# Two private pairs of PSUM banks become one ring of four for the first layer and the attention beside it

## The chip, the cores and the metric

One Trainium2 chip, one of its cores. The metric is device time in microseconds (us): the time of the whole program on that core, median of several executions. Engines are named as the profile names them: PE is TensorE (matmul), PEld its weight load, DVE is VectorE, ACT is ScalarE, SP issues DMAs.

## The reference

Attention with random features for 4 batches, 8 heads and 576 tokens, then two feed-forward layers over all 2304 tokens. Inputs are double precision.

```
def phi(x):
    h = einsum('bhsd,md->bhsm', x, omega) - sum(x * x, -1) / 2
    return exp(h - max(h, -1)) / sqrt(m)
kv  = einsum('bhsm,bhsd->bhmd', phi(k), v);  z = sum(phi(k), axis=2)
x   = (phi(q) @ kv) / (phi(q) @ z + 1e-6)          # to 2304 x 512
h   = x @ w_in                                     # 512 -> 2048
y   = (h * sigmoid(1.702 * h)) @ w_out             # first layer
out = ((y @ w_a) * (y @ w_b)) @ w_out2             # second layer
```

## The kernel before

Every matrix is held as a sum of two half-precision parts, high and low, so a product takes three matmuls (high by high, high by low, low by high). The work runs in this order on one core: the attention of batch 0 alone, then four tiles of 512 tokens of the first layer, then a rest tile of 256 tokens, then the second layer. Beside tile 0 runs the attention of batch 1, beside tile 1 that of batch 2, beside tile 2 that of batch 3. Tile 3 has none beside it. These four stretches are called stages A, B, C and D below.

**A tile of the first layer** (`ffn1`) has 16 h units, numbered f. Unit f is 12 matmuls into one PSUM bank `ph` (L654 to L656), then tanh on ACT (L662, gives `th`), a product on DVE that reads `ph` a second time (L665), a rounding copy on ACT (L671, `gh`) and the rest on DVE (L672, `gl`). The bank is free after L665. Two units later in program order `y_unit` f takes `gh` and `gl` into four accumulators `y` with 12 more matmuls (L685 to L687).

**The attention of a batch** goes by head pairs, k0 to k3 and then q0 to q3 (named k1_2 for batch 1, head pair 2). A pair takes three feature tiles of one PSUM bank `pa` each (L414 and L415: four, four and one slots). From each bank DVE takes the maximum (L480, then L486 makes the bias `nb`), and ACT the exponentials (L446), after which that bank is free. A k pair then sums into one bank of `pa` (L538 and L540 for batch 1, L528 to L530 later) that a copy on ACT empties (L544, or L503 and DVE's L504). A q pair multiplies by that sum (L584) into two banks, which DVE divides (L593 to L598). The attention's matmuls, the weights' conversion (L214, L254, L262 on DVE, L272 on ACT, L221 on DVE) and the h units are written as generators that take turns: `run` steps the tile, then the weights, then `side_step` steps each attention phase that is alive.

**Who sets the order.** The order of instructions on each engine is laid down by the scheduler when the program is built. It goes by the order of the program and by when a tile's buffer comes free: a matmul that opens a bank whose former tenant is not yet read stands behind others that can go. PSUM has eight banks: `ps_acc` holds four for the `y` accumulators, `ps_ring` two for `ph`, `ps_att` two for `pa`. Each of these pools hands out its banks in turn, and each turn waits for that bank's last reader.

```
ps_acc = ctx.enter_context(tc.tile_pool(name="ps_acc", bufs=4, space=PSUM))
ps_ring = ctx.enter_context(tc.tile_pool(name="ps_ring", bufs=2, space=PSUM))
ps_att = ctx.enter_context(tc.tile_pool(name="ps_att", bufs=2, space=PSUM))
```

`head` opens tiles 0 and 1: it takes the first three units, the third into a bank of `ps_acc`.

Of the kernel before, what the change touches and what calls it, by code (L numbers as in the profile page):

```python
# [9 lines left out]
F32 = mybir.dt.float32  # L10
# [23 lines left out]
def fused_kernel(  # L34
# [18 lines left out]
    P = 128  # L53
# [27 lines left out]
    ps_ring = ctx.enter_context(tc.tile_pool(name="ps_ring", bufs=2, space=PSUM))  # L81
    ps_att = ctx.enter_context(tc.tile_pool(name="ps_att", bufs=2, space=PSUM))
# [207 lines left out]
    def w_need(n):  # L290
        while w_done[0] < n:
            w_done[0] = next(w_gen)
# [348 lines left out]
    YS = S_Y / (S_G * S_W)  # L641
    ys = {}

    def ffn1(j, xh, xl, n):

        gh, gl, yacc, phs = {}, {}, {}, {}

        def h_products(f, cs, pool=ps_ring, tag="ring"):
            if f not in phs:
                phs[f] = pool.tile([P, 512], F32, tag=tag, name=f"ph{j}_{f}")  # L650
            ph = phs[f]
            w, fs = w_in[f // 8], slice(f % 8 * P, (f % 8 + 1) * P)
            for c in cs:
                nc.tensor.matmul(ph[:, :n], w[:, 0, c, fs], xh(c), start=(c == 0), stop=False)  # L654
                nc.tensor.matmul(ph[:, :n], w[:, 0, c, fs], xl(c), start=False, stop=False)  # L655
                nc.tensor.matmul(ph[:, :n], w[:, 1, c, fs], xh(c), start=False, stop=(c == KC - 1))  # L656

        def h_unit(f, cs=range(KC)):
            h_products(f, cs)
            ph = phs.pop(f)  # L660
            th = mp.tile([P, 512], F32, tag="f32", name=f"th{j}_{f}")
            nc.scalar.activation(  # L662
                out=th[:, :n], in_=ph[:, :n], func=AF.Tanh, scale=0.5 * 1.702 / (S_X * S_W)
            )
            nc.vector.scalar_tensor_tensor(  # L665
                out=th[:, :n], in0=th[:, :n], scalar=1.0, in1=ph[:, :n], op0=ALU.add, op1=ALU.mult
            )
            GS = 0.5 * S_G / (S_X * S_W)
            a = gp.tile([P, 512], F16, tag="gh", name=f"gh{j}_{f}")
            b = gp.tile([P, 512], F16, tag="gl", name=f"gl{j}_{f}")  # L670
            nc.scalar.activation(out=a[:, :n], in_=th[:, :n], func=AF.Copy, scale=GS)  # L671
            nc.vector.scalar_tensor_tensor(  # L672
                out=b[:, :n], in0=th[:, :n], scalar=GS, in1=a[:, :n],
                op0=ALU.mult, op1=ALU.subtract,
            )
            gh[f], gl[f] = a, b

        def y_unit(f):
            w = w_out[f // 4]
            for c in range(KC):  # L680
                if f == 0:
                    yacc[c] = ps_acc.tile([P, 512], F32, tag="acc", name=f"y{j}_{c}")
                cs = slice(c * P, (c + 1) * P)
                o = yacc[c][:, :n]
                nc.tensor.matmul(o, w[:, 0, f % 4, cs], gh[f][:, :n], start=(f == 0), stop=False)  # L685
                nc.tensor.matmul(o, w[:, 0, f % 4, cs], gl[f][:, :n], start=False, stop=False)  # L686
                nc.tensor.matmul(o, w[:, 1, f % 4, cs], gh[f][:, :n], start=False, stop=(f == FC1 - 1))  # L687

        def main(after=None, first=2):

            following = None
            for f in range(FC1):
                w_need(2 * (f // RW) + 2)
                y_unit(f)
                if f + 1 == FC1:
                    yd = ydram.tile([P, KC, 512], F32, tag=f"y{j}", name=f"yd{j}")
                    for c in range(KC):
                        ye = mp.tile([P, 512], F32, tag="f32", name=f"ye{j}_{c}")
                        nc.scalar.activation(out=ye[:, :n], in_=yacc[c][:, :n], func=AF.Copy, scale=YS)
                        nc.sync.dma_start(out=yd[:, c, :n], in_=ye[:, :n])  # L700
                    ys[j] = yd
                yield
                if first <= f + 2 < FC1:
                    w_need(2 * ((f + 2) // RW) + 1)
                    h_unit(f + 2)
                    yield
                elif f + 2 >= FC1 and after is not None:
                    if following is None:
                        following = after()
                    following[2](f + 2 - FC1)  # L710
                    yield

        return main, h_products, h_unit


# [298 lines left out]


    def psp_att():
        return ps_att.tile([P, 512], F32, tag="att", name="pa")

    rr = [0]

# [94 lines left out]
    def rest_tile():  # L1115
        xTr = zp.tile([P, 2, KC, 2, P], F16, tag="z", name="xTr")
        for r in range(2):
            nc.sync.dma_start_transpose(
                out=xTr[:, :, :, r, :].rearrange("p l c t -> p (l c) t"),
                in_=x16r[:, r].rearrange("p l c t -> p (l c t)"),  # L1120
            )
        return ffn1(
            4,
            lambda c: xTr[:, 0, c].rearrange("p r t -> p (r t)"),
            lambda c: xTr[:, 1, c].rearrange("p r t -> p (r t)"),
            2 * P,
        )
# [2 lines left out]

    def head(tile, units):
        _, products, unit = tile
        for f in range(units):
            w_need(2 * (f // RW) + 1)
            if f < 2:
                products(f, range(KC - 1))
            else:
                products(f, range(KC - 1), ps_acc, "acc")
            yield
        for f in range(units):  # L1140
            unit(f, (KC - 1,))
            yield

    def next_tile(b, make):
        def made():
            finish_side(b)
            following.append(make())
            return following[-1]

        return made  # L1150

    xT = x_tile(0, zp, "z")
    with tc.tile_pool(name="att", bufs=2) as att:
# [28 lines left out]
        with tc.issue_after(own["xt", "q0_2"].ins):  # L1182
            w_steps(POST_W, NW1)
        following.append(ffn1(0, *xparts(xT), SM))
        for b in range(1, B):
            x1 = x_tile(b, zp, "z")
            t0 = (0, 0, 1, -EARLY)[b]
            if b < 3:
                begin_k(b, att, psp_att, t0, AL, b == 1)
            begin_q(b, att, x1, psp_att, t0 + NHP * AL, AL, b == 1)  # L1190
            if b == 2:
                begin_k(3, att, psp_att, 37 - EARLY, AL, False)
            ahead = next_tile(b, lambda: ffn1(b, *xparts(x1), SM))
            if b == 1:
                run(head(following[0], 3), 1, NW1)
                run(following[0][0](first=3), 1, NW1)
                ahead()
            else:
                if b == 2:
                    run(head(following[-1], 3), 11 / 32, NW1 + 2)  # L1200
                run(following[-1][0](ahead, 3 if b == 2 else 2), 11 / 32, (NW1 + 2, NWE)[b - 2])
# [50 lines left out]
```

## Time and profile before

| what | value |
|---|---|
| median of 3 runs | 900.74 us (899.37 to 902.21) |
| the profiled execution | 899.4 us, its span 897.6 us |
| stage A (tile 0, batch 1) | 54.6 to 176.3 us |
| stage B (tile 1, batch 2) | 176.3 to 278.0 us |
| stage C (tile 2, batch 3) | 278.0 to 383.0 us |
| stage D (tile 3 alone) | 383.0 to 468.5 us |
| rest tile and second layer | 468.5 to 897.6 us |
| PE busy | 872.3 us of the span |

The profile is of one execution, 1.3 us below the median of the three. Its span runs from the first instruction to the last. The stage limits are read from the timeline of PE, about where one tile gives way to the next. In the timelines a matmul's length is that of its passage, while the next one starts earlier: matmuls of 512 columns start one after another, at less than their length, so what a matmul costs PE is read from start to start. Of DVE too an instruction starts a little before its forerunner's printed end.

### The profile page before, as it was taken

The page shows a single profiled execution, that of the slowest core. Times are in us where ns is not written, and L with a number is a line of the kernel's source. Part 1 is how long each engine was busy: PE and PEld are TensorE (multiplying, and loading weights), DVE is VectorE, ACT ScalarE, POOL GpSimd, SP SyncE. Part 2 cuts the span into 40 slices and gives each one's busy share as a digit, 9 for nine tenths or more (in the row PEclk, how much of TensorE's full clock was granted, in tenths as well). Part 3 has the DMA queues.
Part 4 walks back from the last instruction along what each step waited for, and adds up shares of the span by engine and source line. Part 5 has one row for each costly group of instructions (what it writes and reads, how often), then busy time and mean ns, then how long its engine had stood idle before and what let it go on. Part 6 is the DMA issues. An engine that isn't in the chain of part 4 may idle for free.

```text
span 897.6 us, 17390 instructions
## 1 busy us (share of the span) xinstructions
PE 872.3 (97%) x7094; PEld 626.3 (70%) x7094; DVE 690.9 (77%) x1244; ACT 455.3 (51%) x1087; POOL 1.4 (0%) x10
## 2 busy tenths in 40 slices
PE   8999999999999999999999999999999999999997
PEld 6864555644554455444448888888888888888886
DVE  5889999778797787999923399777999558566766
ACT  7777774677566776454323354544443122233221
POOL 0000000000000000000000000000000000000000
PEclk9999999999999999999999999999999999999999
DMA  7856895453674323885401055212332022223312
GB/s 205 242 142 162 205 228 197 120 120 82 137 161 110 75 40 67 146 259 222 135 7 49 24 177 175 106 43 83 134 126 83 5 40 84 83 99 125 87 39 71
DMA packets 129343, 105.35 MB, mean 117 GB/s; under 512 B 97776, under 2 KB 111088, under 8 KB 127216
## 3 DMA queue, kind: packets, MB, share of 16 engines
q1 hardware_dynamic: 128558, 103.66, 41.2%
q8 instruction: 55, 0.90, 0.4%
q10 hardware_dynamic: 706, 0.59, 0.2%
q14 instruction: 24, 0.20, 0.1%
HBM read 71.07 MB, written 17.69 MB: 99 GB/s over the span
## 4 chain that ended last, share of the span: by engine, by line
PE 59%; DVE 21%; DMA 7%; ACT 7%; issue 2%; ACTq 0%; SPq 0%; DVEq 0%
PE ph L655 3%; PE ph L654 3%; PE ph L656 3%; PE y L685 3%; PE y L686 3%; PE y L687 3%; DMA xt_k<-x_k 3%; PE oA L904 2%; PE oA L902 2%; PE oA L903 2%; PE pbA L811 2%; PE pbA L809 2%; PE pbA L810 2%; PE paA L809 2%; PE pa L568 2%
## 5 line engine op out<-in xcount | busy, mean ns | idle before, releaser
L686 PE MATMUL y<-gl,w_out 128*128 128x512 f16 (+1 forms) x320 | 114.4, 358 | 0.9 <-DVE gl L672 0.8
L687 PE MATMUL y<-gh,w_out 128*128 128x512 f16 (+1 forms) x320 | 114.2, 358 | 0.0
L685 PE MATMUL y<-gh,w_out 128*128 128x512 f16 (+1 forms) x320 | 111.9, 358 | 0.8 <-ACT gh L671 0.7
L654 PE MATMUL ph<-xT,w_in 128*128 128x512 f16 x256 | 97.1, 379 | 1.5 <-DMA xT<-x_q_3x 0.7
L655 PE MATMUL ph<-xT,w_in 128*128 128x512 f16 x256 | 97.1, 379 | 0.3 <-DVE xT L623 0.3
L656 PE MATMUL ph<-xT,w_in 128*128 128x512 f16 x256 | 97.1, 379 | 0.0
L665 DVE SCALAR_TENSOR_TENSOR th<-th,ph 128x512 f32<-128x512 f32 (+1 forms) x80 | 50.3, 629 | 39.9 <-ACT th L662 39.7
L662 ACT ACTIVATE th<-ph 128x512 f32<-128x512 f32 (+1 forms) x80 | 44.2, 553 | 48.8 <-PE ph L656 48.8
L671 ACT ACTIVATE gh<-th 128x512 f16<-128x512 f32 (+1 forms) x80 | 47.1, 588 | 42.0 <-DVE th L665 41.9
L672 DVE SCALAR_TENSOR_TENSOR gl<-th,gh 128x512 f16<-128x512 f32 (+1 forms) x80 | 50.7, 634 | 15.9 <-ACT gh L671 15.5
L809 PE MATMUL paA<-forms,w_a 128*128 128x256 f16 (+1 forms) x240 | 61.0, 262 | 1.6 <-DVE ca L828 0.8
L809 PE MATMUL pbA<-forms,w_b 128*128 128x256 f16 (+1 forms) x240 | 61.1, 262 | 0.9 <-DVE cb L828 0.9
L811 PE MATMUL pbA<-forms,w_b 128*128 128x256 f16 (+1 forms) x240 | 61.0, 262 | 0.0
L811 PE MATMUL paA<-forms,w_a 128*128 128x256 f16 (+1 forms) x240 | 61.0, 262 | 0.0
L810 PE MATMUL pbA<-forms,w_b 128*128 128x256 f16 (+1 forms) x240 | 61.0, 262 | 0.0
L810 PE MATMUL paA<-forms,w_a 128*128 128x256 f16 (+1 forms) x240 | 61.0, 262 | 0.0
L902 PE MATMUL oA<-w_o,ab 128*128 128x256 f16 x216 | 58.9, 273 | 1.6 <-ACT ab L860 0.9
L904 PE MATMUL oA<-w_o,ab 128*128 128x256 f16 x216 | 58.9, 273 | 0.6 <-DVE ab L861 0.5
L903 PE MATMUL oA<-w_o,ab 128*128 128x256 f16 x216 | 58.9, 273 | 0.0
L817 ACT COPY ka<-paA 128x512 f32<-128x512 f32 (+1 forms) x30 | 16.3, 543 | 78.2 <-PE paA L811 78.1
L910 DVE SCALAR_TENSOR_TENSOR o<-oA,o 128x512 f32<-128x512 f32 (+1 forms) x45 | 28.5, 633 | 34.2 <-PE oA L904 34.2
L687 PEld LDWEIGHTS <-w_out 128*128 128x128 f16 x320 | 31.4, 98 | 29.9 <-issue 3.0
(209 smaller groups left out, 2353.5 us busy)
## 6 DMA issues: line engine op xcount, KB each, us to landing
wraw<-in_moe_w_out_dram SPq DMA_DIRECT2D x14, 1024.0 KB
forms<-fd SPq DMA_DIRECT2D x8, 1792.0 KB
wraw<-in_moe_w_in_dram SPq DMA_DIRECT2D x8, 1024.0 KB
fd<-forms SPq DMA_DIRECT2D x4, 1792.0 KB
wraw<-in_moe_w_a_dram SPq DMA_DIRECT2D x6, 1024.0 KB
wraw<-in_moe_w_b_dram SPq DMA_DIRECT2D x6, 1024.0 KB
vt<-in_v_dram SPq DMA_DIRECT2D x16, 256.0 KB
rawq<-in_q_dram SPq DMA_DIRECT2D x16, 256.0 KB
```

What stands on the lines that cost most here:

```text
L654: nc.tensor.matmul(ph[:, :n], w[:, 0, c, fs], xh(c), start=(c == 0), stop=False)
L655: nc.tensor.matmul(ph[:, :n], w[:, 0, c, fs], xl(c), start=False, stop=False)
L656: nc.tensor.matmul(ph[:, :n], w[:, 1, c, fs], xh(c), start=False, stop=(c == KC - 1))
L685: nc.tensor.matmul(o, w[:, 0, f % 4, cs], gh[f][:, :n], start=(f == 0), stop=False)
L686: nc.tensor.matmul(o, w[:, 0, f % 4, cs], gl[f][:, :n], start=False, stop=False)
L687: nc.tensor.matmul(o, w[:, 1, f % 4, cs], gh[f][:, :n], start=False, stop=(f == FC1 - 1))
L809: nc.tensor.matmul(o[:, i], wh, xh, start=first, stop=False, skip_group_check=True)
L810: nc.tensor.matmul(o[:, i], wh, xl, start=False, stop=False, skip_group_check=True)
L811: nc.tensor.matmul(o[:, i], wl, xh, start=False, stop=final, skip_group_check=True)
L902: nc.tensor.matmul(bank[:, t], lh, wh, start=first, stop=False, skip_group_check=True)
L903: nc.tensor.matmul(bank[:, t], lh, wl, start=False, stop=False, skip_group_check=True)
L904: nc.tensor.matmul(bank[:, t], ll, wh, start=False, stop=final, skip_group_check=True)
```

## The change

`shared()` counts the allocations and hands them to the two pools in turn: the first to `ps_att`, the next to `ps_ring`, and so on. The h units of all tiles and the attention tiles of batches 1 to 3 draw from it, so that the two pairs become one ring of four banks, taken in the order of the program. While `head` runs, `apart[0]` is set and each kind takes its own pool as before. The sums of k pairs and q pairs draw from it too, since they are made by the same `psp_att`. Nothing else is edited. Lines from 641 on move down: L654 to L656 become L667 to L669, L662 L675, L665 L678, L671 L684, L672 L685, L685 to L687 L698 to L700.

```diff
+    taken, apart = [0], [False]
+
+    def shared(own_pool, own_tag, name):
+
+        pool, tag = own_pool, own_tag
+        if not apart[0]:
+            taken[0] += 1
+            pool, tag = ((ps_ring, "ring"), (ps_att, "att"))[taken[0] % 2]
+        return pool.tile([P, 512], F32, tag=tag, name=name)
+
     def ffn1(j, xh, xl, n):
...
-        def h_products(f, cs, pool=ps_ring, tag="ring"):
+        def h_products(f, cs, pool=None, tag=None):
             if f not in phs:
-                phs[f] = pool.tile([P, 512], F32, tag=tag, name=f"ph{j}_{f}")
+                if pool is None:
+                    phs[f] = shared(ps_ring, "ring", f"ph{j}_{f}")
+                else:
+                    phs[f] = pool.tile([P, 512], F32, tag=tag, name=f"ph{j}_{f}")
...
     def psp_att():
-        return ps_att.tile([P, 512], F32, tag="att", name="pa")
+        return shared(ps_att, "att", "pa")
...
     def head(tile, units):
         _, products, unit = tile
+        apart[0] = True
...
         for f in range(units):
             unit(f, (KC - 1,))
             yield
+        apart[0] = False
```

The instructions of both kernels are the same in kind and number on every engine; their order differs. Three places are shown. In the names `th0_4` is unit 4 of tile 0, `mx_k1_2_1` the maxima of batch 1, head pair 2, first group.

DVE in stage A, from `gl` of unit 3 to `gl` of unit 4 of tile 0, before (`wf` is a weight chunk in conversion):

```order
L672 SCALAR_TENSOR_TENSOR gl0_3_1122<-th0_3_1118,gh0_3_1121 128x512
L486 SCALAR_TENSOR_TENSOR nb_k1_1_1_1039<-mh_k1_1_1_1038,sq_k1_1_910 128x4
L262 SCALAR_TENSOR_TENSOR wf5_1080<-wraw5_897,wf5_1080 128x1024
L214 TENSOR_SCALAR wf6_1300<-wraw6_1027 128x1024
L480 TENSOR_REDUCE mx_k1_1_2_1082<-pa_1086 128x1
L665 SCALAR_TENSOR_TENSOR th0_4_1228<-th0_4_1228,ph0_4_1215 128x512
L486 SCALAR_TENSOR_TENSOR mh_k1_1_2_1083<-mx_k1_1_2_1082,sq_k1_1_910 128x5
L254 SCALAR_TENSOR_TENSOR wf6_1300<-wraw6_1027,wf6_1300 128x1024
L486 SCALAR_TENSOR_TENSOR nb_k1_1_2_1084<-mh_k1_1_2_1083,sq_k1_1_910 128x5
L672 SCALAR_TENSOR_TENSOR gl0_4_1232<-th0_4_1228,gh0_4_1231 128x512
```

The same stretch after the change, of whose 25 rows between the two the last ten are shown:

```order
L685 SCALAR_TENSOR_TENSOR gl0_3_1122<-th0_3_1118,gh0_3_1121 128x512
...
L480 TENSOR_REDUCE mx_k1_3_1_1257<-pa_1196 128x4
L486 SCALAR_TENSOR_TENSOR mh_k1_2_2_1190<-mx_k1_2_2_1189,sq_k1_2_977 128x5
L214 TENSOR_SCALAR wf7_1443<-wraw7_1237 128x1024
L486 SCALAR_TENSOR_TENSOR nb_k1_2_2_1191<-mh_k1_2_2_1190,sq_k1_2_977 128x5
L486 SCALAR_TENSOR_TENSOR mh_k1_3_1_1258<-mx_k1_3_1_1257,sq_k1_3_1067 128x4
L254 SCALAR_TENSOR_TENSOR wf7_1443<-wraw7_1237,wf7_1443 128x1024
L486 SCALAR_TENSOR_TENSOR nb_k1_3_1_1259<-mh_k1_3_1_1258,sq_k1_3_1067 128x4
L221 SCALAR_TENSOR_TENSOR w_in0_87<-wf6_1300,w_in0_87 128x4x256
L678 SCALAR_TENSOR_TENSOR th0_4_1228<-th0_4_1228,ph0_4_1215 128x512
L262 SCALAR_TENSOR_TENSOR wf7_1443<-wraw7_1237,wf7_1443 128x1024
L685 SCALAR_TENSOR_TENSOR gl0_4_1232<-th0_4_1228,gh0_4_1231 128x512
```

The product `th0_4` has moved from the fifth place behind `gl0_3` to the 24th. The 25 rows between `gl0_3` and `gl0_4` are 9 of L486, 3 of L480 over 512 elements, 2 of L480 over 128, 7 of the weights' 128x1024 operations with two inputs (L254, L262, L221), 2 of L214, 1 of L403 and 1 of L678. Before, it was 8 rows: 3 of L486, 1 of L480 over 128, 2 with two inputs, 1 of L214 and 1 of L665. On PE, from the first matmul with `gl0_3` to the one with `gl0_4`, there are now 21 matmuls of 512 columns, 34 of 128 columns (L414, L415) and the sums of two k pairs (L538, L540); before it was 22, 2 and none.

PE in stage C, from the last matmul of unit 5 of tile 2 to the first that takes its `gh2_5`, before (rows that repeat are left out):

```order
L656 MATMUL ph2_5_4040<-xT2_2210,w_in0_87 128x512
L685 MATMUL y2_0_3698<-gh2_4_3916,w_out1_90 128x512
L686 MATMUL y2_0_3698<-gl2_4_3917,w_out1_90 128x512
...
L654 MATMUL ph2_6_4173<-xT2_2210,w_in0_87 128x512
...
L414 MATMUL pa_4027<-om_h_93,xt_k3_3_3858 128x128
...
L414 MATMUL pa_4088<-om_h_93,xt_k3_3_3858 128x128
...
L656 MATMUL ph2_6_4173<-xT2_2210,w_in0_87 128x512
...
L656 MATMUL ph2_6_4173<-xT2_2210,w_in0_87 128x512
L685 MATMUL y2_0_3698<-gh2_5_4056,w_out1_90 128x512
L686 MATMUL y2_0_3698<-gl2_5_4057,w_out1_90 128x512
```

And after:

```order
L669 MATMUL ph2_5_4040<-xT2_2210,w_in0_87 128x512
L700 MATMUL y2_3_3710<-gh2_4_3916,w_out1_90 128x512
L528 MATMUL pa_4119<-v16_k3_1_4062,e16_k3_1_3689 128x130
...
L528 MATMUL pa_4119<-v16_k3_1_4062,e16_k3_1_3689 128x65
...
L530 MATMUL pa_4119<-v16_k3_1_4062,e16_k3_1_3689 128x65
L414 MATMUL pa_4157<-om_h_93,xt_k3_3_3858 128x128
...
L414 MATMUL pa_4160<-om_h_93,xt_q3_0_3970 128x128
...
L698 MATMUL y2_0_3698<-gh2_5_4056,w_out1_90 128x512
L698 MATMUL y2_1_3702<-gh2_5_4056,w_out1_90 128x512
...
L699 MATMUL y2_0_3698<-gl2_5_4057,w_out1_90 128x512
```

Before, 24 matmuls of 512 columns and 18 of 128 columns stand between; now one of 512 columns, the 27 of a k pair's sum (L528 to L530) and 10 of 128 columns. The four products with `gh2_5` now come one after another ahead of the first with `gl2_5`.

ACT in stage C, around the tanh and the rounding copy of that unit, before:

```order
L503 ACTIVATE kvh_97<-pa_3986 128x130
L662 ACTIVATE th2_5_4053<-ph2_5_4040 128x512
L518 ACTIVATE v16_k3_2_4195<-vt_133 128x2x260
L518 ACTIVATE v16_k3_2_4195<-vm_134 128x2x65
L671 ACTIVATE gh2_5_4056<-th2_5_4053 128x512
```

And after:

```order
L402 ACTIVATE x16_q3_2_4231<-rawq_3_2_4170 128x9x64
L446 ACTIVATE e_k3_3_0_4083<-pa_4027,nb_k3_3_1_4079 128x128 x4
L675 ACTIVATE th2_5_4053<-ph2_5_4040 128x512
L430 ACTIVATE rawq_3_2_4170<-rawq_3_2_4170 128x576
L684 ACTIVATE gh2_5_4056<-th2_5_4053 128x512
L456 ACTIVATE e16_k3_3_3854<-e_k3_3_0_4083 128x512
```

Between tanh and copy stood two conversions of values and now stands one square (L430); ahead of the tanh there now stand the exponentials of the next head pair.

## Rows read from the trace of the kernel before

**Rows 1.** The page, part 1: busy time, share of the span, count of PE, PEld, DVE, ACT, POOL.
```profile
PE 872.3 (97%) x7094; PEld 626.3 (70%) x7094; DVE 690.9 (77%) x1244; ACT 455.3 (51%) x1087; POOL 1.4 (0%) x10
```

**Rows 2.** Busy time by stage A, B, C, D: window, length, engines (count), clock, DMA share, GB/s.
```profile
54.60:176.30 121.70, 117.64 (x730) 66.89 (x730) 110.56 (x196) 83.38 (x290) 0.00 (x0) 1.00 0.65 176
176.30:278.00 101.70, 98.36 (x742) 50.72 (x741) 84.11 (x195) 71.21 (x176) 0.00 (x0) 1.00 0.59 128
278.00:383.00 105.00, 101.74 (x758) 52.23 (x756) 83.70 (x193) 67.82 (x168) 0.00 (x0) 1.00 0.42 91
383.00:468.50 85.50, 83.93 (x387) 37.61 (x385) 67.86 (x104) 36.07 (x60) 0.00 (x0) 1.00 0.48 157
```

**Rows 3.** Waits of PE, from stages A, B, C, D: waited for, us in total, times, longest.
```profile
PE pa L414 <- ACT e_k L446: 1.7, 1, 1.7
...
PE pa L528 <- DVE sx L248: 0.8, 1, 0.8
...
PE pa L584 <- DMA eqT_q<-e_q: 1.0, 1, 1.0
...
PE ph L654 <- DMA xT<-x_q_3x: 0.7, 1, 0.7
```

**Rows 4.** Timeline of DVE in stage A: start us, length us, line, operation, tiles, shape, count.
```profile
77.49 0.75 DVE L403 SCALAR_TENSOR_TENSOR x_q<-rawq,x_q 128x576 f16<-128x576 f32 x1
...
81.38 0.16 DVE L486 SCALAR_TENSOR_TENSOR nb_k<-mh_k,sq_k 128x4 f32<-128x4 f32 x1
81.45 1.22 DVE L262 SCALAR_TENSOR_TENSOR wf<-wraw,wf 128x1024 int32<-128x1024 int32 x1
82.59 0.69 DVE L214 TENSOR_SCALAR wf<-wraw 128x1024 int32<-128x1024 int32 x1
83.19 0.28 DVE L480 TENSOR_REDUCE mx_k<-pa 128x1 f32<-128x128 f32 x1
83.39 0.68 DVE L665 SCALAR_TENSOR_TENSOR th<-th,ph 128x512 f32<-128x512 f32 x1
...
92.10 0.68 DVE L480 TENSOR_REDUCE mx_k<-pa 128x4 f32<-128x512 f32 x1
```

**Rows 5.** Timeline of PE in stage A, same columns, the wait before an instruction in brackets.
```profile
78.82 0.22 PE L414 MATMUL pa<-om_h,xt_k 128*128 128x128 f16 x1 [1.75 <-ACT e_k L446]
78.88 0.22 PE L415 MATMUL pa<-om_l,xt_k 128*128 128x128 f16 x1
...
82.09 0.38 PE L686 MATMUL y<-gl,w_out 128*128 128x512 f16 x1
82.30 0.38 PE L687 MATMUL y<-gh,w_out 128*128 128x512 f16 x1
...
88.31 1.90 PE L540 MATMUL pa<-vt,e_k 128*128 128x65 f32 x16
90.04 0.38 PE L685 MATMUL y<-gh,w_out 128*128 128x512 f16 x1
```

**Rows 6.** Timeline of PE, then of ACT, around one h unit of stage D.
```profile
450.10 0.38 PE L656 MATMUL ph<-xT,w_in 128*128 128x512 f16 x1
...
450.52 0.60 ACT L662 ACTIVATE th<-ph 128x512 f32<-128x512 f32 x1 [3.36 <-PE ph L656]
...
451.87 0.63 ACT L671 ACTIVATE gh<-th 128x512 f16<-128x512 f32 x1 [0.76 <-DVE th L665]
```

**Rows 7.** Timeline of ACT around one h unit of stage C.
```profile
327.15 0.62 ACT L662 ACTIVATE th<-ph 128x512 f32<-128x512 f32 x1
...
328.76 1.14 ACT L446 ACTIVATE e_q<-pa,nb_q 128x128 f32<-128x128 f32 x4 [0.42 <-DVE nb_q L486]
329.87 0.63 ACT L671 ACTIVATE gh<-th 128x512 f16<-128x512 f32 x1
```

**Rows 8.** Timeline of PE in stage C: first and last matmul of one k-phase sum.
```profile
340.37 0.22 PE L528 MATMUL pa<-v_k,e_k 128*128 128x130 f16 x1 [0.22 <-ACT e_q L446]
...
341.25 0.19 PE L530 MATMUL pa<-v_k,e_k 128*128 128x65 f16 x1
```

## The prediction

> **What bounds the kernel now.** I read the page first: PE is busy for 872.3 us of a span of 897.6, all other engines far less [rows 1]. Then busy time by stage. The change touches stages A to D alone, and there PE is idle for 121.70 − 117.64 = 4.06 us in A, 3.34 in B, 3.26 in C and 1.57 in D, together 12.2 us, at a granted clock of 1.00 in all four [rows 2]. This is a lower bound: matmuls of 512 columns start every 0.215 us while each is printed as 0.38 long (82.09 and 82.30) [rows 5], so a printed matmul covers 0.16 us of a gap behind it. The second thing to see there is DVE: 110.56 us busy of 121.70 in A, so A has two engines near their end, while B and C leave DVE 17 to 21 us. Then PE's waits [rows 3]: few, single, and from different causes. No one wait repeats through a stage.
>
> The profiled execution took 899.4 us, 1.3 below the median of 900.74. The sum is made against 899.4 and 1.3 is added back. A measurement of this kernel can tell about 0.3%, 2.7 us, from no change.
>
> **What the change removes and adds.** No instruction is added or removed, and no DMA; the cost is only in order and waits. The edit of the allocation does three things: it lets attention tiles be opened when both banks of their old pair are unread, it makes an h unit stand behind attention tiles that it never met before, and so it pulls the attention ahead of the h units on PE and on DVE.
>
> *Stage A, unit 4 of tile 0.* The first place shown in the order: between `gl0_3` and `gl0_4` DVE had 8 rows and has 25. From start to start [rows 4] L486 takes 0.07, a two-input 128x1024 operation 82.59 − 81.45 = 1.14, L214 0.60, L480 over 128 elements 0.20; of L403, L665 and L480 over 512 I take the length less the 0.08 that the others overlap: 0.67, 0.60, 0.60. The sum is 9 × 0.07 + 7 × 1.14 + 2 × 0.60 + 2 × 0.20 + 3 × 0.60 + 0.67 + 0.60 = 13.3 us, and 0.68 for `gl0_4`, of L665's shape. DVE is through with `gl0_3` at 81.38 [rows 4] in either kernel, as nothing of the first layer has moved ahead of it, so `gl0_4` is there at 81.4 + 14.0 = 95.4. PE takes `gl0_3` at 82.09, or at 81.5 at the earliest, and then has 21 matmuls of 0.215, 34 of 0.06 (78.82 to 78.88) and two k sums of 1.73 (88.31 to 90.04) and a little more [rows 5]: 10.0 to 10.4 us. It arrives between 91.5 and 92.5 and stands until 95.4. The stall is 2.9 to 3.9; I take **+3.2**. Every matmul behind it waits, since all the work that could be pulled ahead has been.
>
> What hides part of it: batch 1 is through its attention earlier, so DVE is less pressed at the end of the stage. The 1.75 us wait for the exponentials [rows 5] lies before the place, and what it may save is lost again at `gl0_4`. Of the waits behind it I give back 0.7, so A is **+2.5**; the ends are 0 (all 3.2 made up in the stage) and +3.9.
>
> *Stages B and C, the cover of an h unit.* The second place: unit 5 of tile 2 had 24 × 0.215 + 18 × 0.06 = 6.2 us of PE work between its last matmul and the first that takes `gh`. It has now 0.215 + 10 × 0.06 + the k sum, 341.25 − 340.37 + 0.03 = 0.91 [rows 8]: 1.7 us. By the same count units 6 and 7 of that tile have 1.9 and 1.4, and unit 8 of tile 1 has 1.9; units 5 and 6 of tile 1 have 2.5 and 2.7, and the others over 2.8. The chain that has to fit in it is read in stage D, where nothing disturbs it: last matmul at 450.10, so its successor is due at 450.32, and `gh` is written at 451.87 + 0.63 = 452.50 [rows 6], 2.2 us. In stage C it was longer, 327.15 to 330.50 from tanh to copy, 3.35 against 1.98, as exponentials of 1.14 stood between [rows 7], that is 3.6 with the 0.2 ahead of it. At 2.2 the shortfalls of tile 2 are 0.5 + 0.3 + 0.8 = 1.6 us, and of tile 1 0.3. At 3.6 they are 1.9 + 1.7 + 2.2 = 5.8, and 1.7 + 1.1 + 0.9 = 3.7. The third place, ACT's order, shows between tanh and copy only a square of the size of a copy, which DVE's product covers, so I stand near the lower end: C **+2.4**, B **+0.9**. The `gl` are no further loss, as four products with `gh` (0.86) now go ahead of the first with `gl`.
>
> *New waits of the ring.* A matmul that opens an attention bank now waits 15 times for DVE's L678, behind which the next attention tile and all of PE are queued; by the same count four of the 15 have 1.0 to 1.4 us of work against the 1.5 from 450.32 to the end of the product in stage D (tanh at 450.52, copy at 451.87) [rows 6], a shortfall of 1.2 in all. Eleven times an h unit waits for exponentials, with 2.2 us of work or more. Nothing of this is in the trace of before: the ends are 0 and about 3 us, twice the shortfall and some for the exponentials. I take **+1.0**.
>
> *Waits that go.* A k sum (L528) waited 0.8 in B, its cover now being 5 us and more where it was 2 to 3; L584 waited 1.0 in C for the transposed exponentials [rows 3], and these are ready earlier: **−1.8**, 0 at worst. At the start of D a matmul waited 0.7 for the last transposed tile [rows 3]; batch 3 is through some 7 us of PE work sooner: **−0.7**. What might be late next there is DVE, at 67.86 of 85.5 us [rows 2], which I cost at nothing.
>
> The sum: 2.5 + 0.9 + 2.4 + 1.0 − 1.8 − 0.7 = +4.3 by these terms. Each shortfall is taken alone, though a PE that has stood once comes later to the next, and I strike off about a quarter: **+3.3**. That is 902.7 for the profiled execution and **904.0** for the median.
>
> **A rule against this reading.** PE's waits are single and differ [rows 3]; on that I rest the view that more banks have little to give. The Trainium skill, Perfetto Trace Analysis, section Optimization Strategy, says that the same gap repeated on the engine that should be saturated can mean too little PSUM for the next tile. By that rule the ring would take out the gaps; as no gap repeats in a stage here, the trace does not bear it out, and I give it no more than the first rival's chance.
>
> **The rivals.**
>
> *Faster: the bank waits go and the new order holds.* An h unit and the attention each have bursts, and four banks in one ring lend to whichever has one. For it: 12.2 us of idle PE, of which the listed waits that open or close a bank or come behind one are 1.7 + 0.8 + 1.0 + 0.7 = 4.2. Against it: the DVE queue of stage A. If the stall at unit 4 is made up in the same stage (A at −1.7 + 0), chains stay at 2.2 (B and C at +1.9) and the ring's waits are 0, it comes to −1.7 + 1.9 − 2.5 = −2.3, and −4.2 if the shortfalls are covered by PE's being late: 896.5 to 898.4 for the median. It decides if PE's work per stage, which is the same in both, absorbs the stall: PE then waits early and not late.
>
> *No change.* The stall of 3.2 in A replaces other waits of A (4.06 idle in all), and B and C lose 1.9 and win 1.8: 899.5 to 902.5, about 901.
>
> *Slower by more.* Chains in B and C at 3.6 [rows 7] (+9.5), stage A at +3.9, the ring at +3, against −2.5: about +14 at the outside; half the long chains give +9, about **911**. It needs ACT's exponentials to stand ahead of each tanh; they do ahead of unit 5 in the third place.
>
> *The clock falls.* All four stages are at a granted clock of 1.00, 2.4 GHz, with a wait of 1.75 us among them [rows 2, 5], so stalls of 3 us need not lower it. If it fell to 1.2 GHz for 20 us of matmuls, that stretch would take 20 more: about 920. The Trainium skill, TensorE: Matmul & The Clock Gate, section A second HAM failure mode: psum-queue depth-cycling, tells of a kernel whose PE idled between groups as PSUM banks cycled, and whose clock went up and down; the granted clock of before shows none of it [rows 2].
>
> **How the numbers follow.** The forecast, +0.5 to +7 (901.2 to 908), has 0.47; the faster rival 0.21; no change 0.21; slower by more 0.09; the clock 0.02. Of the forecast 0.09 lies below 903.4 and counts as the same. So faster 0.21, same 0.30, slower 0.49. The range leaves out the clock, the far end of the slower rival and the lowest part of the faster: 897 to 911, around 904.0.
>
> **What would show it.** Right: PE idle of some 3 us ahead of `y` of unit 4 of tile 0, released by DVE's L685 or ACT's L684; waits of L698 for L684 in stage C; stage A 2 to 3 us longer, C 1 to 2; no wait of L528 or L584; stage D 0.7 shorter; rest the same. Wrong: stage A as long as before, or no wait at L698. If D or the second layer moved by over 1 us, the cause would be one that I have not named.

## The result and the profile after

| | median | lowest to highest | executions |
|---|---|---|---|
| before | 901.01 us | 899.37 to 902.21 | 4 |
| after | 911.29 us | 906.14 to 916.32 | 4 |

The ratio is 1.0116 (95% interval 1.0094 to 1.0139): 10 us slower. The forecast was 904.0, in a range up to 911. The spread is new too: 10 us between executions where the kernel before has 3. The profiled execution is the quickest of the four, 906.14 us with a span of 904.3; it shows less than the whole loss.

The page of the changed kernel: busy time, then PE and PEclk in 40 slices.

```profile
PE 872.4 (96%) x7094; PEld 629.2 (70%) x7094; DVE 689.2 (76%) x1244; ACT 456.4 (50%) x1087; POOL 1.4 (0%) x10
...
PE   8987899999999999999999999999999999999997
...
PEclk9999999999999999999999999999999999999999
```

PE's work is what it was [rows 1], so the 6.7 us that this span is longer are gaps and slow matmuls. The third, fourth and fifth slices of PE (45 to 113 us) have lost busy time; PEclk, in tenths over 22.6 us, shows nothing yet. Now by stage; each limit lies at the same distance from the tile's last `y` product as before, and the columns are those of [rows 2].

```profile
54.60:184.20 129.60, 118.57 (x730) 68.18 (x728) 114.35 (x204) 90.27 (x300) 0.00 (x0) 0.99 0.65 175
184.20:285.70 101.50, 98.31 (x742) 51.41 (x741) 81.75 (x192) 68.21 (x171) 0.00 (x0) 1.00 0.57 120
285.70:389.00 103.30, 100.26 (x757) 52.87 (x755) 85.66 (x194) 66.63 (x166) 0.00 (x0) 1.00 0.51 113
389.00:475.30 86.30, 84.39 (x389) 37.71 (x388) 62.80 (x98) 34.20 (x55) 0.00 (x0) 1.00 0.36 124
```

Stage A is 129.60 us and was 121.70: +7.9. B is −0.2, C −1.7, D +0.8 [rows 2]. PE is idle for 11.03 us in A where it was for 4.06, and its clock there has a mean of 0.99. So stage A carries all of it. The waits of PE in A, over the stretch of the same limits as before:

```profile
PE pa L538 <- ACT e_k L446: 4.7, 2, 2.9
PE pa L414 <- DMA xt_k<-x_k: 2.0, 1, 2.0
PE pa L414 <- ACT e_k L446: 1.6, 2, 1.1
...
```

The first row was not there before, nor the second; the third is about the one of [rows 3]. Stage D has a row that grew from 0.8 us:

```profile
PE y L699 <- DVE gl L685: 1.8, 4, 0.5
```

**The place.** PE's timeline in tile 0, a wait in brackets:

```profile
81.89 0.38 PE L699 MATMUL y<-gl,w_out 128*128 128x512 f16 x1
...
83.85 0.38 PE L700 MATMUL y<-gh,w_out 128*128 128x512 f16 x1
87.18 0.49 PE L538 MATMUL pa<-vm,e_k 128*128 128x130 f32 x2 [2.95 <-ACT e_k L446]
...
89.40 0.31 PE L414 MATMUL pa<-om_h,xt_k 128*128 128x128 f16 x1
89.51 0.31 PE L415 MATMUL pa<-om_l,xt_k 128*128 128x128 f16 x1
...
90.89 0.27 PE L414 MATMUL pa<-om_h,xt_k 128*128 128x128 f16 x1 [0.43 <-ACT e_k L446]
...
91.05 0.63 PE L667 MATMUL ph<-xT,w_in 128*128 128x512 f16 x1
91.48 0.63 PE L668 MATMUL ph<-xT,w_in 128*128 128x512 f16 x1
...
92.83 0.38 PE L669 MATMUL ph<-xT,w_in 128*128 128x512 f16 x1
93.05 0.38 PE L667 MATMUL ph<-xT,w_in 128*128 128x512 f16 x1
...
96.23 0.49 PE L538 MATMUL pa<-vm,e_k 128*128 128x130 f32 x2 [1.72 <-ACT e_k L446]
...
99.40 0.38 PE L699 MATMUL y<-gl,w_out 128*128 128x512 f16 x1
```

At 83.85 PE has done the products of unit 3. Next in its queue is a sum of k pair 0 (L538), which opens a bank of the ring whose former tenant is a feature tile of k pair 1. It waits 2.95 us for that tile's exponentials. ACT's timeline:

```profile
77.92 1.37 ACT L446 ACTIVATE e_k<-pa,nb_k 128x128 f32<-128x128 f32 x5
...
83.53 0.68 ACT L402 ACTIVATE x_q<-rawq 128x576 f16<-128x576 f32 x1 [0.51 <-DMA xt_k<-x_k]
84.11 1.04 ACT L272 ACTIVATE w_out<-wf 128x1024 f16<-128x1024 f32 x1
85.06 0.24 ACT L422 ACTIVATE rawk<-rawk 128x64 f32<-128x64 f32 x1
...
86.01 1.37 ACT L446 ACTIVATE e_k<-pa,nb_k 128x128 f32<-128x128 f32 x5
...
94.55 0.60 ACT L675 ACTIVATE th<-ph 128x512 f32<-128x512 f32 x1 [0.51 <-PE ph L669]
```

and DVE's, whose bias for them is the first row:

```profile
83.71 0.16 DVE L486 SCALAR_TENSOR_TENSOR nb_k<-mh_k,sq_k 128x5 f32<-128x5 f32 x1
...
91.30 0.89 DVE L480 TENSOR_REDUCE mx_k<-pa 128x1 f32<-128x128 f32 x2 [1.96 <-PE pa L415]
...
95.27 0.68 DVE L678 SCALAR_TENSOR_TENSOR th<-th,ph 128x512 f32<-128x512 f32 x1
...
97.46 0.69 DVE L685 SCALAR_TENSOR_TENSOR gl<-th,gh 128x512 f16<-128x512 f32 x1 [0.37 <-ACT gh L684]
```

Pair 0's own exponentials had ended at 79.29 (the row of 77.92), so the sum does not wait for its own data: it waits for the bank. The bias of pair 1 was there at 83.87. ACT's queue had a conversion ahead of the exponentials that stood 0.51 us for a DMA, a rounding copy of a weight chunk of 1.04 us and four squares; they began at 86.01, and at 87.18 L538 could go.

They are no later than before, however. The same places in the kernel before, PE and then ACT:

```profile
84.66 0.38 PE L656 MATMUL ph<-xT,w_in 128*128 128x512 f16 x1
...
86.60 0.38 PE L656 MATMUL ph<-xT,w_in 128*128 128x512 f16 x1
...
88.03 0.44 PE L538 MATMUL pa<-vm,e_k 128*128 128x130 f32 x2
```

```profile
86.42 1.37 ACT L446 ACTIVATE e_k<-pa,nb_k 128x128 f32<-128x128 f32 x5
```

There the five exponentials began at 86.42 and the first k sum at 88.03, without a wait, since PE had products of an h unit and of `y` to make until then. With the ring the next h products stand behind the attention's banks and begin at 91.05. So the ring did not make the exponentials late; it took away the work that had covered them.

The second k sum waits 1.72 us at 96.23 for exponentials that stand on ACT behind the tanh of 94.55, which itself waits for PE. The product `th0_4` runs at 95.27 and `gl0_4` at 97.46, late as forecast and later, but PE takes `gl0_4` only at 99.40, with no wait: the stalls ahead of it in PE's own queue have used up the time. DVE, which I had working without a gap, itself stood 1.96 us at 91.30 for PE.

**The clock.** In the same rows matmuls of 128 columns start 0.11 us apart from 89.40, and those of 512 columns 0.43 apart at 91.05, against 0.22 at 92.83. The busy time and clock of these stretches:

```profile
84.00:89.00 5.00, 2.05 (x18) 1.82 (x17) 5.00 (x8) 4.57 (x25) 0.00 (x0) 1.00 0.62 213
89.00:93.00 4.00, 3.57 (x20) 2.26 (x20) 2.04 (x8) 2.29 (x7) 0.00 (x0) 0.57 0.12 24
```

Ahead of it PE had been busy for 2.05 of 5 us. Then the granted clock is at its lower level, 1.2 GHz, from about 89 to about 92.5. That stretch costs half its length, some 1.7 us. In the other executions the mean clock is lower: 0.992, 0.992 and 0.986 for 911.32, 911.25 and 916.32 us. With (1 − clock) × span taken off, the four come to 904.3, 904.0, 904.0 and 903.5. So what differs between them is, to 0.8 us, the clock.

### The profile page after: what moved, and what is told of

Read it like the earlier page. It is cut to its first block, busy times and chain, and to the rows that moved or that the text cites. A ratio compares the mean times of both kernels' runs of the same rounds, so it can differ in the third digit from the quotient of the medians.

```text
span 904.3 us, 17397 instructions
## 1 busy us (share of the span) xinstructions
PE 872.4 (96%) x7094; PEld 629.2 (70%) x7094; DVE 689.2 (76%) x1244; ACT 456.4 (50%) x1087; POOL 1.4 (0%) x10
## 4 chain that ended last, share of the span: by engine, by line
PE 59%; DVE 26%; ACT 6%; issue 3%; DMA 3%; ACTq 0%; DVEq 0%; SPq 0%
PE y L699 4%; PE y L698 4%; PE ph L667 4%; PE ph L668 3%; PE ph L669 3%; PE y L700 3%; PE oA L917 2%; PE oA L915 2%; PE oA L916 2%; PE pbA L822 2%; PE pbA L824 2%; PE pbA L823 2%; PE paA L822 2%; DVE gl L685 2%; PE paA L824 2%
## 5 line engine op out<-in xcount | busy, mean ns | idle before, releaser
L699 PE MATMUL y<-gl,w_out 128*128 128x512 f16 (+1 forms) x320 | 114.2, 358 | 2.9 <-DVE gl L685 2.7
L700 PE MATMUL y<-gh,w_out 128*128 128x512 f16 (+1 forms) x320 | 114.3, 358 | 0.0
L698 PE MATMUL y<-gh,w_out 128*128 128x512 f16 (+1 forms) x320 | 110.3, 357 | 1.8 <-ACT gh L684 1.6
L678 DVE SCALAR_TENSOR_TENSOR th<-th,ph 128x512 f32<-128x512 f32 (+1 forms) x80 | 50.5, 631 | 66.6 <-ACT th L675 66.4
L667 PE MATMUL ph<-xT,w_in 128*128 128x512 f16 x256 | 97.3, 380 | 1.5 <-ACT e_q L446 0.9
L669 PE MATMUL ph<-xT,w_in 128*128 128x512 f16 x256 | 97.3, 380 | 0.0
L675 ACT ACTIVATE th<-ph 128x512 f32<-128x512 f32 (+1 forms) x80 | 44.2, 552 | 79.8 <-PE ph L669 78.8
L685 DVE SCALAR_TENSOR_TENSOR gl<-th,gh 128x512 f16<-128x512 f32 (+1 forms) x80 | 50.8, 636 | 17.7 <-ACT gh L684 17.2
L684 ACT ACTIVATE gh<-th 128x512 f16<-128x512 f32 (+1 forms) x80 | 47.0, 588 | 31.4 <-DVE th L678 30.7
L700 PEld LDWEIGHTS <-w_out 128*128 128x128 f16 x320 | 31.3, 98 | 32.9 <-issue 6.0
```

## The experiments

**The change once more.** No edit.

> The changed kernel once more, unedited, for more executions and a second profile. Theory (every execution loses the same 3 us by waits, and the rest by the clock): time plus or minus 0.7 us is 904 + (1 - granted clock) x 909, and in the profile every stretch with a clock under 1.00 lies in stage A behind a stall of PE. Rival (the spread is not the clock's): times of one clock differ by over 2 us, or the low clock lies elsewhere.

Measured: 910.9 us (908.56 to 912.31), ratio 1.0115 (1.0085 to 1.0144). The second profile has the same waits (2.93 and 1.72 at the k sums) and one low stretch, at the same place. By the same subtraction its four executions come to 903.2 to 905.8, up to 1.8 us from the 904 expected where 0.7 was allowed; the clock column has three digits only, and one unit of the last is 0.9 us. Not all of the spread is the clock's: stage C takes 105.3 us in the second profile and 103.3 in the first, both at a clock of 1.00. Over the eight executions of the change the clock takes 6.7 us on average and the rest is 904.2; over 13 of the kernel before it takes 1.7 and the rest is 898.6. Of the 10.6 us between these means some 5.6 are waits and order, then, and some 5 the clock. Where the clock was low in the executions without a profile is not shown.

**The ring without stage A.**

```diff
-    taken, apart = [0], [False]
+    taken, apart, ring = [0], [False], [False]
...
-        if not apart[0]:
+        if ring[0] and not apart[0]:
...
                 ahead()
+                ring[0] = True
```

> The ring is off while tile 0 and batch 1 run (stage A keeps the two pairs) and on from stage B. Theory (the cost is stage A: waits for banks of the ring and a lower clock behind them): stage A as before, granted clock 1.00 throughout, B to D together 0 to 2 us shorter than before, so 899 to 902 us. Rival (the covers of the h units in B and C cost as forecast, 2 to 3 us, and the clock falls there too): 903 us or more. Rival (no part of it matters alone, only the whole): 906 or more.

Measured: 899.03 us, ratio 0.9989 (0.9973 to 1.0005), clock 0.998 to 1.000. From stage B on the ring costs nothing that can be told.

**The ring in stage A alone.** The same flag, the other way round: set at first, cleared behind `ahead()`.

> The ring is on in stage A alone; from tile 1 and batch 2 on the two pairs are back. Theory (stage A is the cost): as slow as the change, 905 to 917 us, granted clock 0.985 to 0.999, tile 0 over some 8 us later than before. Rival (B and C carry the cost): within 2 us of before.

Measured: 913.22 us (909.79 to 920.64), ratio 1.0154 (1.0102 to 1.0206), clock 0.984 to 0.998. Stage A is the cost. Its profiled execution, the slowest and above the range expected, shows a low clock at three places. The first, at some 15 to 33 us, is in batch 0's attention and the last, at 285 us, in tile 1 with the two pairs, neither of which the ring touches; only the second, from 104 us, lies in stage A. There it came behind the second k sum's wait of 1.72 us, and not behind the first's of 2.93.

**PE kept at work where it stood.** Zero weights, so that nothing is added.

```diff
                 y_unit(f)
+                if j == 0 and f == 3:
+                    for i in range(11):
+                        nc.tensor.matmul(
+                            yacc[i % KC][:, :n], own["zero"][:, 0], xh(0), start=False, stop=False
+                        )
...
```

> The change, with eleven matmuls of 512 columns more, zero weights added into the open y accumulator of tile 0 before the last product of unit 3: 2.4 us of PE work where PE stood for 3 us before the first k sum of batch 1; they wait for nothing and add nothing to the result. Theory (the clock falls because PE stood idle there): granted clock 0.998 or more in every run, 903 to 906 us, although there is more work. Rival (the clock falls for another cause, or by the many short gaps around): clock and time as the change, 906 to 917. Rival (the stall is not waiting but lack of order): time up by the 2.4 us.

Measured: 908.42 us (905.21 to 909.99), ratio 1.0085 (1.0054 to 1.0116), clock 0.993 to 0.998. The wait at the first k sum fell from 2.95 to 0.59 us. Its windows, around the first and behind the second k sum:

```profile
84.00:95.00 11.00, 7.85 (x51) 4.72 (x50) 9.33 (x18) 9.17 (x45) 0.00 (x0) 1.00 0.51 148
...
96.00:101.00 5.00, 5.00 (x35) 3.71 (x35) 3.37 (x9) 3.56 (x14) 0.00 (x0) 0.66 0.98 369
```

The clock stays up where it had fallen, and falls some 8 us later, behind the second k sum, whose 1.72 us were left. So the time is in the range of the rival, 906 to 917, and the clock short of the 0.998 expected, though this profile shows the first fall gone. With more of them:

```diff
+                if j == 0 and f == 4 and c == KC - 1:
+                    for i in range(8):
...
+                if j == 0 and f in (2, 3):
+                    for i in range({2: 5, 3: 11}[f]):
...
```

> The change with 24 zero-weight matmuls of 512 columns (5.2 us of PE work) spread over the three places of tile 0 where PE stood longest in the two profiles of the change: five at the end of unit 2's products, eleven at the end of unit 3's, eight behind unit 4's h products. Theory (the lower clock follows from PE's standing in this stretch): granted clock like that of the kernel before, 0.997 to 1.000, in every run, and 903 to 907 us, below the 911 of the change, though it does more work. Rival (the lower clock comes from elsewhere): clock 0.986 to 0.998 as in the change, and 911 us or more.

Measured: 909.35 us (908.0 to 910.52), ratio 1.01 (1.0085 to 1.0115), clock 0.994 to 0.998. The windows, the first of them in batch 0's attention:

```profile
8.00:12.00 4.00, 4.00 (x30) 3.35 (x31) 2.54 (x6) 1.49 (x3) 0.00 (x0) 0.57 0.87 193
78.00:84.00 6.00, 5.52 (x44) 3.17 (x43) 5.65 (x11) 5.03 (x27) 0.00 (x0) 1.00 0.62 190
84.00:92.00 8.00, 7.47 (x55) 4.82 (x54) 7.50 (x13) 6.61 (x32) 0.00 (x0) 1.00 0.47 147
92.00:102.00 10.00, 7.91 (x58) 5.16 (x57) 9.17 (x16) 7.68 (x36) 0.00 (x0) 1.00 0.92 265
```

No low clock is left in stage A in the profile, and by the clock column the four executions lose 3.4 us on average where the change loses 6.7. The result lies between the theory, 903 to 907, and its rival, 911 and more: 24 products of 0.215 are 5.2 us, of which only part fell into waits; without the clock's part the mean is 905.9 against 904.2. That all the 5 us of the clock would be got back by filling the gaps is not shown.

Where the clock falls can be read from all 14 profiles, leaving out the last 3 us of each, where the program ends. Each of the 15 low stretches in them begins behind a wait of PE of 1.4 to 4.0 us: 11 in stages A to D, and four in batch 0's attention. But not each such wait is followed by one. In stages A to D, of seven waits of 2.9 us or more at the full clock five were, and of 22 waits between 1.3 and 2.6 us six.

**The ring from the q phase of batch 1.** I took the k sums for the cause.

```diff
         nc.scalar.copy(own["kv"][:, hp], pk)
+        if (b, hp) == (1, NHP - 1):
+            ring[0] = True
...
```

> The two pairs are kept until the last k sum of batch 1 is made; from the q phase of batch 1 on there is the ring. Theory (what costs is the k sums of batch 1, which stand in the ring ahead of h units 4 to 6): the first half of tile 0 as before, time 899 to 903 us, granted clock as before. Rival (the ring costs throughout stage A, wherever DVE is pressed): 904 us or more.

Measured: 923.99 us (921.74 to 925.42), ratio 1.0261 (1.0243 to 1.0279), the slowest of all: the theory that only the k sums cost fell. Up to unit 4 tile 0 runs as before, and its last product comes 23 us later. PE in that stretch:

```profile
126.89 0.27 PE L414 MATMUL pa<-om_h,xt_q 128*128 128x128 f16 x1 [0.97 <-ACT e_q L446]
...
134.10 0.59 PE L669 MATMUL ph<-xT,w_in 128*128 128x512 f16 x1 [5.09 <-ACT e_q L446]
```

ACT:

```profile
126.70 0.29 ACT L565 COPY eT_q<-pa 128x128 f32<-128x128 f32 x1
131.02 1.06 ACT L272 ACTIVATE w_in<-wf 128x1024 f16<-128x1024 f32 x1 [4.03 <-DVE wf L262]
...
132.94 1.37 ACT L446 ACTIVATE e_q<-pa,nb_q 128x128 f32<-128x128 f32 x5
```

PE by stretch, with clock:

```profile
112.00:117.00 5.00, 0.44 (x6) 0.15 (x2) 4.79 (x8) 1.89 (x6) 0.00 (x0) 0.72 0.79 228
117.00:126.00 9.00, 7.98 (x47) 7.28 (x48) 5.46 (x9) 5.97 (x29) 0.00 (x0) 0.50 0.79 259
126.00:134.00 8.00, 2.12 (x10) 1.91 (x10) 7.96 (x13) 3.97 (x19) 0.00 (x0) 0.50 0.69 136
```

The first matmul of an h unit (L669 in this kernel) stands behind an unread q tile for 5.09 us. ACT's queue is held for 4.03 us by the rounding copy of a weight chunk, which waits for DVE's conversion; the exponentials that free the bank stand behind it, at 132.94. Their own bias came from DVE only at 131.1, so ACT's queue accounts for the last 1.8 us of their delay; the rest lies ahead of the bias. And PE, idle for most of this, does its next work at half clock. By the clock column the four executions lose 14.8 us to the clock, more than half of the 24. It is the same chain as in the change, at a q phase: the ring puts an h unit behind an attention bank, and that bank behind whatever ACT and DVE have queued. The change from pairs to ring in mid-stage is this run's own, so it shows that a q phase can be hit, not what the q phase costs in the change, where the waits of A for `e_q` are 0.5 us and less.

**Spacing.** If crowding is the cause, beginning batch 1's head pairs further apart should help. `AL`, 2 turns from one pair to the next, becomes 3, 4 or 5 for batch 1 (shown for 4):

```diff
-                begin_k(b, att, psp_att, t0, AL, b == 1)
-            begin_q(b, att, x1, psp_att, t0 + NHP * AL, AL, b == 1)
+                begin_k(b, att, psp_att, t0, 4 if b == 1 else AL, b == 1)
+            begin_q(b, att, x1, psp_att, t0 + NHP * (4 if b == 1 else AL), 4 if b == 1 else AL, b == 1)
```

> The change, with the head pairs of batch 1 begun every third turn in place of every second. Theory (the stall is that too much of batch 1's k phase is allocated between two h units): the stall of 2.9 us ahead of the first k sum under 1 us, time 899 to 904 us, granted clock as before. Rival (the ring itself, with h units behind unread attention banks, costs at any spacing): stage A 5 us or more longer than before, 905 to 916 us.

> The same with every fourth turn. Theory: the k phase's stalls are gone as with every third turn, but the q phase of batch 1 ends later, up to eight turns, and tile 1 may wait for it: 899 to 906 us. Rival: as with every third turn.

> The ring with batch 1 begun every fifth turn. Theory (what counts is that the attention's banks and the h units alternate evenly over the tile; at four the attention of batch 1 ends just ahead of tile 1): the start of tile 1 waits for the last transposed tile of batch 1, 898 to 905 us. Rival (wider is better still): under 895 us.

> The ring with batch 1 begun every fourth turn once more, on the chip of its control. Theory: 894 to 898 us, under the kernel before by 2 to 6 us. Rival (the earlier result was the chip's): within 1.5 us of before.

And the same edit on the kernel before, with its pairs:

> The kernel before with its two pairs, and batch 1 begun every fourth turn: the control for the ring spaced by four (895.9 us). Theory (spacing alone spreads batch 1's k phase, and with pairs it cannot fill the gaps it leaves): 898 to 903 us, so that ring and spacing are faster together by 2 us or more. Rival (the gain is the spacing's alone, the ring gives nothing): 894 to 897 us. Rival (pairs need the close spacing): over 903 us.

| turns between head pairs of batch 1 | banks | median | ratio to before (95%) |
|---|---|---|---|
| 2 | pairs (before) | 900.0 to 901.0 in four comparisons | |
| 4 | pairs | 906.06 | 1.0067 (1.0049 to 1.0085) |
| 2 | ring (the change) | 911.29 | 1.0116 (1.0094 to 1.0139) |
| 3 | ring | 899.42 | 0.9993 (0.9981 to 1.0005) |
| 4 | ring | 895.87 | 0.9969 (0.9948 to 0.9990) |
| 4, once more | ring | 895.78 | 0.9948 (0.9932 to 0.9964) |
| 5 | ring | 906.79 | 1.0073 (1.0050 to 1.0095) |

With the ring, one more turn takes the loss away, as expected. Two make the kernel faster than before, below the 899 that I had taken for the least. Tile 0 and batch 1 with the ring and four turns, up to just behind the tile's last product:

```profile
54.60:166.50 111.90, 110.70 (x694) 64.06 (x693) 104.11 (x180) 78.45 (x277) 0.00 (x0) 1.00 0.66 191
```

111.90 us where before had 121.70 [rows 2] and the change 129.60, with 1.20 us of PE idle. Most of the difference is not won: the window has 110.70 us of PE work where before had 117.64, and the rest of batch 1 comes behind it, at the start of tile 1, where a wait for a transposed tile of batch 1 is 1.8 us. At the first `y` product of tile 1 the gain is 4.1 us, and PE's idle time up to there is 3.4 us against 4.8. With pairs, four turns are too wide: batch 1 ends later and tile 1 waits for it, and the clock falls behind that wait.

```profile
184.83 0.53 PE L654 MATMUL ph<-xT,w_in 128*128 128x512 f16 x1 [4.00 <-DMA xT<-x_q_3x]
```

```profile
178.00:184.00 6.00, 2.44 (x12) 1.09 (x12) 4.95 (x12) 3.07 (x6) 0.00 (x0) 1.00 0.29 49
184.00:189.00 5.00, 4.17 (x19) 2.16 (x19) 2.06 (x4) 3.43 (x6) 0.00 (x0) 0.66 0.83 177
```

The profile shows a second fall, at 308 us in stage C, behind a wait of 1.96 us for DVE. So the ring alone costs 10 us, the spacing by four alone 5, and both together win 4 to 5. Pairs spaced by three were not tried, so whether some spacing helps without the ring is open. At five turns the ring loses as well, and not where I expected it. In tile 0 an h product waits 2.90 us for exponentials of a k pair (76.61), and near the start of tile 1 two transposes of batch 1's q pairs (L561) wait 4.6 us together; the clock falls behind both places. By the clock column it takes 7.0 us of these executions and 1.6 of those of the kernel before, which is most of the loss.

**All batches spaced.** Batches 2 and 3 every third turn besides:

```diff
-                begin_k(b, att, psp_att, t0, AL, b == 1)
-            begin_q(b, att, x1, psp_att, t0 + NHP * AL, AL, b == 1)
+                begin_k(b, att, psp_att, t0, 4 if b == 1 else 3, b == 1)
+            begin_q(b, att, x1, psp_att, t0 + NHP * (4 if b == 1 else 3), 4 if b == 1 else 3, b == 1)
```

> The ring with batch 1 begun every fourth turn and batches 2 and 3 every third. Theory (in stages B and C the ring costs nothing, so their spacing has little to give): 893 to 899 us. Rival (the same crowding costs in B and C too): under 893 us. Rival (their attention ends too late): over 900 us.

Measured: **892.09 us** (891.31 to 892.30), ratio 0.9904 (0.9889 to 0.9919), the best here and 8.7 us faster than before. That is in the range of the rival, that crowding costs in B and C too: my theory gave them too little. Its waits of PE, stages A to D, the two largest:

```profile
PE ph L667 <- DMA xT<-x_q_3x: 3.0, 2, 1.8
PE ph L667 <- DMA xT<-x_q_2x: 2.9, 1, 2.9
...
```

What waits now are the starts of tiles 1, 2 and 3 for the last transposes of the batch before. The wait of 2.9 us, at tile 3, left the clock at 1.00. Other spacings of batches 2 and 3, with pairs among them, were not tried.

## Why the prediction was wrong

**The direction and the stage** were right: slower, and stage A the largest term, though by its own sum hardly larger than C (2.5 against 2.4). What was wrong is the size, 3.3 forecast against 10. (The slower rival's 911 is mis-added by a little: 900.7 and 9 make 909.7.)

**Stage A, unit 4 of tile 0** is the step that failed. I had PE arrive at `gl0_4` between 91.5 and 92.5 and stand there until 95.4. `gl0_4` was done at 98.15, and of the 2.75 us that this is later, 2.33 are DVE's own waits, for PE and ACT, where I had it work without a gap. But PE's 10 us of work on the way were taken at their durations only. From its first product with `gl0_3` (81.89) to the one with `gl0_4` (99.40) it took 17.5: the 10 of work, waits of 2.95, 0.43 and 1.72, and some 1.7 for the clock. The two long waits are the k sums', which I had among the work at 1.73 us each. Each opens a bank, and its former tenant's exponentials come when they came before, while the h products that used to cover them now stand behind. My term for new waits of the ring had attention banks that wait for L678 and h units that wait for exponentials; a k sum that waits for exponentials is in neither. The idle time of PE in A rose by 7.0 us against a term of 2.5. That the loss would partly be made up in the stage did not happen within it either; a wait for the DMA of a transposed k (2.0, at 66.75) came on top. It is in each profile that has the ring from the start of stage A with head pairs two turns apart, and in no other; its cause was not followed further.

**The clock** is the second step, and about half the loss. I wrote that a wait of 1.75 us with the clock at 1.00 meant that stalls of 3 us need not lower it, and gave it 0.02. In both profiles of the change it fell behind the 2.9 us wait, in the one with eleven zero products behind the next, in the pairs spaced by four behind 4.00 us at tile 1, and in stages A to D of none of the profiles of the ring spaced by three or four. That a single wait need not lower it holds all the same: two of the seven waits of 2.9 us or more did not. So the error was the chance. My price had been 20 us once; it was 5 on average, 1.7 in one profile. The mean clock of the change is 0.986 to 0.998 against 0.995 to 1.000. The Trainium skill, TensorE: Matmul & The Clock Gate, section A second HAM failure mode: psum-queue depth-cycling, tells of a kernel whose PE idles between groups of matmuls often as it goes round the PSUM banks, and whose clock goes up and down with it. I cited it and set it aside because the kernel before showed none of it. The runs here agree in part: the clock falls behind PE's idling for a bank, but after one or two single waits in a stage, and behind waits for a DMA too (the 4.00 us).

**Stages B, C and D** were forecast at +0.9, +2.4, −0.7 with +1.0 for waits and −1.8 for those that go, in all +1.8. They are −0.2, −1.7 and +0.8 in the profile (−0.1, +0.3 and +0.8 in the second profile of the change), and with the ring from stage B alone the whole is 0.9989 of before. The waits of L698 for L684 that I took from the cover of units 5 to 8 came to 0.5 in B and 0.2 in C. The waits of L528 went, as forecast; that of L584 changed its cause and stayed at 0.9 in C. In D the wait of 0.7 went, and `gl` more than took it back: 1.8 us of L699 against 0.8, which I had costed at nothing.

**The rule on repeated gaps** was set aside with the argument that the waits of before are single, and more banks have little to give. The rule itself was not tested, as no gap repeats here [rows 3]. The Trainium skill, Perfetto Trace Analysis, section Optimization Strategy, speaks of the same gap repeating for a stretch. But the conclusion that I drew was too strong: with batch 1 spaced by four, the kernel with the ring is 4 to 9 us faster than before; without it, the ring gave the opposite.

## What to carry to other kernels

When a ring is shared in order of allocation, list every instruction that opens a bank, those that only sum included, and ask for each who reads the former tenant last, what stands ahead of that reader in its engine's queue, and what work is left to cover the wait. Sharing buffers and the spacing of the work that fills them are one choice: try them together, since here the ring alone and a spacing by four alone were slower and both together faster. Where a change makes PE stand for a few microseconds at a time, count the granted clock as part of the price, and look at several executions, since the profiled one may be the mildest.

## What the runs showed of the hardware

The clock's part differs from one execution to the next of one kernel with the same waits in its two profiles: mean 0.998 to 0.986, which is 2 to 13 us. Each low stretch in the 14 profiles, ahead of the program's end, begins behind a wait of PE of 1.4 to 4.0 us: in the first profile of the change the wait ends at 87.18 and matmuls slow down from 89.40, in the pairs spaced by four the wait of 4.00 us ends at 184.83 with the clock falling at once. Yet the length of a wait does not settle it: 2.93 us were followed by a fall in one profile (the change once more) and not in another (the ring in stage A alone), at the same k sum. And in four profiles, the fastest kernel's among them, the clock is low in the attention of batch 0, somewhere between 8 and 33 us, behind waits of 1.6 to 1.9 us; that this is part of the 3 us of spread of the kernel before is likely but not shown, as its one profile has no low stretch there.
